# Splitting g tiles one and two points ahead of their products, and deferring parts of w_in's sums, in a fused attention, MoE and gated-layer kernel

## The chip, the cores and the metric

The kernel runs on one core of one Trainium2 chip. The metric is device time in microseconds (us) for one launch; lower is better.

## The reference, cut to what matters

```
kv  = einsum('bhsd,bhse->bhde', k, v);  o = einsum('bhsd,bhde->bhse', q, kv)   # B=8 H=8 S=576 D=64
x   = o / rms(o) * g_norm               # laid out as 4608 rows of 512
e   = argmax(x @ w_gate)                # one of 8 experts for each row
x   = gate_w * (relu(x[e] @ w1[e]) @ w2[e])          # 512 -> 1024 -> 512
h   = x @ w_in                          # 512 -> 2048
g   = h * cos(h)
out = g @ w_out                         # 2048 -> 512, float32
```

## The kernel before, in words

**Precision.** A float32 operand is split in two fp32r tiles, a high part (a ScalarE copy, which rounds) and a low part (the value minus the high part). A product is three passes: high by high, high by low, low by high, as the constant `PASS` says.

**Stages.** The attention part and the routing fill the first 138 us of the trace. The experts r = 0 to 7 follow, in order of size (`emit_f1`, `emit_f2`; L289 and L302 are their matmuls, L291 and L292 the two evictions of the first). From about 677 us on comes the last layer, here called the second half.

**Conversions under the experts.** `w_in` and `w_out` come as 64-bit words. `prep_unit` turns one 128x512 piece into its high and low parts in three steps: VectorE takes exponent and mantissa apart, ScalarE scales (L861, L863), GpSimd multiplies (L864, L865). The generator `prep_units` is advanced one step by each `prep()`, and `prep()` stands between the experts' tiles. The layer with `w_in` uses seven products for a 2x2 block product (sums and differences of blocks take the place of an eighth), so `w_in` also needs four sums per pair of pieces: GpSimd makes them (L886 to L889), ScalarE copies their high parts (L894), VectorE subtracts for the low parts (L895), and GpSimd's queue stores them to `win` in DRAM (L896). This happens eight times, for c = 0 to 7.

**The second half.** A step (p, q) works on a pair p of 512-row groups ("quads") and a block of 2x128 hidden columns. Pair 0 has four steps on one quad, with matmuls of 256 columns; pairs 1 to 4 have eight steps each on two quads: 36 steps in all. In a step TensorE runs the seven products `emit_prod(p, q, 0..6)` (L1174, six 512-column matmuls each from pair 1 on), into the three banks of `ph` and the one of `pt`. VectorE adds them up to four h tiles, C22, C11, C21 and C12 (L1271 to L1310; ScalarE copies product 0 at L1260 and product 4 at L1294, GpSimd adds the latter at L1295). `emit_cos` reduces the argument on VectorE (L1185, L1186, L1188) and takes the cosine on ScalarE (L1190, L1191); `emit_g` multiplies (L1194).

A finished g tile is kept in one of 19 `gslots` until its turn in the list `gq`. From pair 1 on, `gq` takes C11 and C21 of all eight q, for the first quad of the pair, and then C22 and C12, for the second. There are four points in each step, behind products 1, 3, 5 and 6. At each, `emit_split()` takes the next tile of `gq`, if its g is there: ScalarE writes the high part to `gg` (L1207), VectorE the low part (L1208). `second()` right behind it emits the tile's twelve matmuls with `w_out` (L1222). `gg_ring` has three entries. When a quad has all its terms, `emit_rows` copies its four 128-row results out of PSUM (L1233, L1235) and scatters them to `out` (L1236).

All engines run in the order in which the program is written (`manual_schedule`). GpSimd's queue carries the loads of `wi` (L990, five ring entries) and `wo` (L999, four) besides its arithmetic; a load stands behind the product that frees its entry. In the last step of a pair `y_split` makes the operands of the next pair, two ScalarE copies (L971) and two GpSimd subtractions (L972) for each product.

Of the kernel before, what the change touches and what calls it, by code (L numbers as in the profile page):

```python
# [8 lines left out]
F32 = mybir.dt.float32  # L9
# [4 lines left out]
AF = mybir.ActivationFunctionType  # L14
ALU = mybir.AluOpType
# [17 lines left out]
def fused_kernel(  # L33
# [13 lines left out]
    nc = tc.nc  # L47
    P = 128
    B, H, S, D = q.shape
    NT, DM = out.shape  # L50
# [28 lines left out]
    win = dram.tile([C2 // 2, P, 7, 2, 2, P], F32, name="win")  # L79
# [42 lines left out]
    def load_q(b):  # L122
# [24 lines left out]
        out=tri8, in0=iota_e[:, :, None].to_broadcast([P, E, E]),  # L147
        in1=iota_e[:, None, :].to_broadcast([P, E, E]), op=ALU.is_gt)
# [69 lines left out]
    def split_plain(t, d, engine=nc.vector):  # L218
        nc.scalar.activation(d[:, 0], t, AF.Copy)
        engine.tensor_tensor(out=d[:, 1], in0=t, in1=d[:, 0], op=ALU.subtract)  # L220
# [604 lines left out]
    def next_cd():  # L825
        n_cd[0] += 1
        return cds[(n_cd[0] - 1) % len(cds)]

    def prep_unit(i):
        load_raw()  # L830
        t = raws[i]
        d = next_cd()
        if not wide:
            split_plain(t, d)
            yield
            yield
            yield
            return d
        w = t.bitcast(I32).rearrange("p (n two) -> p n two", two=2)
        lo, hi = w[:, :, 0], w[:, :, 1]  # L840
        ex = cpool.tile([P, 512], I32, tag="c0", name="c0")
        nc.vector.tensor_scalar(out=ex, in0=hi, scalar1=0x7FF00000, scalar2=None,
                                op0=ALU.bitwise_and)
        sc = cpool.tile([P, 512], I32, tag="c1", name="c1")
        nc.vector.tensor_scalar(out=sc, in0=hi, scalar1=3, scalar2=0x3F800000,
                                op0=ALU.logical_shift_left, op1=ALU.bitwise_and)
        yield
        nc.vector.scalar_tensor_tensor(out=sc, in0=hi, scalar=-0x40000000, in1=sc,
                                       op0=ALU.bitwise_and, op1=ALU.bitwise_or)
        ef = cpool.tile([P, 512], F32, tag="c2", name="c2")  # L850
        nc.vector.scalar_tensor_tensor(out=ef, in0=ex, scalar=float(0x38100000),
                                       in1=sc.bitcast(F32), op0=ALU.is_ge, op1=ALU.mult)
        nc.vector.tensor_scalar(out=ex, in0=hi, scalar1=9, scalar2=0x7FF,
                                op0=ALU.logical_shift_right, op1=ALU.bitwise_and)
        yield
        nc.vector.tensor_scalar(out=sc, in0=hi, scalar1=0x1FF, scalar2=15,
                                op0=ALU.bitwise_and, op1=ALU.logical_shift_left)
        nc.vector.scalar_tensor_tensor(out=sc, in0=lo, scalar=17, in1=sc,
                                       op0=ALU.logical_shift_right, op1=ALU.bitwise_or)
        mf = cpool.tile([P, 512], F32, tag="c3", name="c3")  # L860
        nc.scalar.activation(mf, ex, AF.Copy, scale=2.0 ** -11, bias=1.0)  # L861
        ml = cpool.tile([P, 512], F32, tag="c4", name="c4")
        nc.scalar.activation(ml, sc, AF.Copy, scale=2.0 ** -35)  # L863
        nc.gpsimd.tensor_tensor(out=d[:, 0], in0=mf, in1=ef, op=ALU.mult)  # L864
        nc.gpsimd.tensor_tensor(out=d[:, 1], in0=ml, in1=ef, op=ALU.mult)  # L865
        yield
        return d


    def prep_units():  # L870
        G = nc.gpsimd
        for c in range(C2 // 2):
            da = yield from prep_unit(2 * c)
            db = yield from prep_unit(2 * c + 1)
            wa = cpool.tile([P, 2, 256], F32, tag="c3", name="wa")
            wb = cpool.tile([P, 2, 256], F32, tag="c4", name="wb")
            for d, w in ((da, wa), (db, wb)):
                G.tensor_tensor(out=w.rearrange("p a n -> p (a n)"), in0=d[:, 0].bitcast(F32),
                                in1=d[:, 1].bitcast(F32), op=ALU.add)
            for d, slots in ((da, (0, 4)), (db, (None, 5))):  # L880
                for h, o in enumerate(slots):
                    if o is not None:
                        G.dma_start(win[c][:, o].rearrange("p t k f -> p t (k f)"),
                                    d.bitcast(F32)[:, :, 256 * h:256 * h + 256])
            yield
            G.tensor_tensor(out=wb[:, 1], in0=wb[:, 0], in1=wb[:, 1], op=ALU.add)  # L886
            G.tensor_tensor(out=wb[:, 0], in0=wa[:, 0], in1=wb[:, 0], op=ALU.subtract)
            G.tensor_tensor(out=wa[:, 0], in0=wb[:, 1], in1=wa[:, 0], op=ALU.subtract)
            G.tensor_tensor(out=wa[:, 1], in0=wa[:, 1], in1=wa[:, 0], op=ALU.subtract)  # L889
            yield  # L890
            for i, w in enumerate((wa, wb)):
                sd = next_cd().rearrange("p t n -> p (t n)").rearrange(
                    "p (a t n) -> p a t n", a=2, t=2)
                nc.scalar.activation(sd[:, :, 0], w, AF.Copy)  # L894
                nc.vector.tensor_tensor(out=sd[:, :, 1], in0=w, in1=sd[:, :, 0], op=ALU.subtract)  # L895
                G.dma_start(  # L896
                    (win[c][:, 2:4] if i else win[c][:, 1:7:5]).rearrange("p a t k f -> p a (t k f)"),
                    sd.bitcast(F32).rearrange("p a t n -> p a (t n)"))
            yield
        for i in range(C2):  # L900
            d = yield from prep_unit(C2 + i)
            G.dma_start(wout[i], d.bitcast(F32))
# [99 lines left out]
    gq, wo_seq = [], []  # L1002
    for q in range(NQ // 2):
        for names, fs in ((("C22", "C21"), (2 * q + NQ, 2 * q + 1 + NQ)),
                          (("C11", "C12"), (2 * q, 2 * q + 1))):
            n = len(wo_seq)
# [138 lines left out]
    reg2_s.close()  # L1145
    reg4 = ctx.enter_context(tc.tile_pool(name="reg4", bufs=1, reuse_waits="tile"))
    wk2 = ctx.enter_context(tc.tile_pool(name="wk2", bufs=2, reuse_waits="tile"))
    gslots = [reg4.tile([P, 512], F32, name=f"g{i}") for i in range(19)]
    stage2 = [reg4.tile([P, 512], F32, name=f"y{i}") for i in range(4)]
    wo = [reg4.tile([P, 2, 512], F32R, name=f"wo{i}") for i in range(WO)]  # L1150
    gg_ring = [reg4.tile([P, 2, 512], F32R, name=f"gg{i}") for i in range(3)]
# [43 lines left out]
        ready.add(key)  # L1195

    n_split = [0]
    waiting = []

    def emit_split():  # L1200
        u = gq[n_split[0]] if n_split[0] < len(gq) else None
        if u is None or u["key"] not in ready:
            return
        gg = gg_ring[n_split[0] % len(gg_ring)]
        n_split[0] += 1
        t = gs.pop(u["key"])
        nc.scalar.activation(gg[:, 0], t, AF.Copy)  # L1207
        nc.vector.tensor_tensor(out=gg[:, 1], in0=t, in1=gg[:, 0], op=ALU.subtract)  # L1208
        gslots.append(t)
        waiting.append((u, gg))  # L1210

    def emit_g2(u, gg, ts=range(4)):
        g = u["g"]
        if g not in acc:
            acc[g] = [ps_a("acc") for _ in range(4)]
        for col, t, item in u["cols"]:
            if t not in ts:
                continue
            wv = wo[item % WO]
            for a, b in PASS:  # L1220
                n = hits[g, t] = hits.get((g, t), 0) + 1
                nc.tensor.matmul(acc[g][t], lhsT=gg[:, a, col * P:(col + 1) * P],  # L1222
                                 rhs=wv[:, b, :], start=(n == 1), stop=(n == 3 * C2))
            if hits[g, t] == 3 * C2:
                emit_rows(g, t)
        if 3 in ts:
            for _ in range(u["n_wo"]):
                load_wo()

    def emit_rows(g, t):  # L1230
        o = wk2.tile([P, DM], F32, tag="yo", name="oo", bufs=4)
        if t % 2:
            nc.scalar.activation(o, acc[g][t], AF.Copy)  # L1233
        else:
            nc.vector.tensor_copy(o, acc[g][t])  # L1235
        sc = nc.gpsimd.indirect_dma_start(  # L1236
            out=out, out_offset=bass.IndirectOffsetOnAxis(
                ap=ctok[:, 4 * g + t:4 * g + t + 1], axis=0),
            in_=o, in_offset=None)
        tc.declare_no_dep(sc.ins, group="rows",  # L1240
                          reason="the rows are a permutation: no two scatters share one")
        tc.add_to_no_dep_group("rows", sc.ins)
        nc.gpsimd.memset(spare, 0.0)

    def second():
        if waiting:
            emit_g2(*waiting.pop(0))

    prev = None
# [79 lines left out]
    second()  # L1329
    emit_g(prev + ("C12",))  # L1330
    while n_split[0] < len(gq):
        emit_split()
        if n_split[0] < len(gq) and len(waiting) > 1:
            second()
    while len(waiting) > 2:
        second()
    for i, ts in ((0, (0, 1)), (1, (0, 1)), (0, (2,)), (1, (2,)), (0, (3,)), (1, (3,))):
        emit_g2(*waiting[i], ts)

# [28 lines left out]
```

## Time and profile before

| | |
|---|---|
| median of three runs | 1836.54 us (1829.53 to 1836.8) |
| the profiled execution | 1835.83 us, its span 1834.0 us |
| busy | PE 1479.6, DVE 1108.8, ACT 662.3, POOL 743.5 us |
| granted TensorE clock, mean | 0.911 |

PE is TensorE (matmul), DVE is VectorE, ACT is ScalarE, POOL is GpSimd. A row of the line table or of the timeline gives line, engine, operation, `output<-inputs`, shape and count; `[2.87 <-ACT gg L1207]` says that the engine sat idle for 2.87 us before it and that this instruction ended the wait. Matmuls overlap, so the ends shown for them are modelled; their starts are read.

### The profile page before, as it was taken

The numbers are of one execution on the slowest core, as the hardware profiler recorded it, in microseconds if no ns is written. First come the engines' busy times: TensorE is split into PE (matmuls) and PEld (weight loads), VectorE is DVE, ScalarE is ACT, GpSimd is POOL, SyncE is SP. The second block draws the span as 40 slices with busy tenths as digits, with TensorE's granted clock in tenths as the row PEclk, the third lists the DMA queues.
The fourth block names the chain that finished last, engine by engine and source line by source line (L and its number), as shares of the span: only waits on it lengthen the run. The fifth ranks groups of instructions, "written<-read, shape, count | busy, mean of one in ns | idle before, by whom it ended". The sixth has DMA issues, their size and how long they took to land.

```text
span 1834.0 us, 22411 instructions
## 1 busy us (share of the span) xinstructions
PE 1479.6 (81%) x7959; PEld 1238.1 (68%) x7959; DVE 1108.8 (60%) x1848; ACT 662.3 (36%) x1308; POOL 743.5 (41%) x869
## 2 busy tenths in 40 slices
PE   7977989989899986677766588886887876888888
PEld 6867879879898985565555466664655655566666
DVE  3987656656788815556666556555555654655651
ACT  5863334434444432323323323233322323323331
POOL 1445456766765652642133412325313334122122
PEclk9989989999999997889887799887989888998999
DMA  9954446656666667465443444544545443445435
GB/s 326 346 178 142 125 155 203 188 161 203 192 217 209 197 182 218 140 200 160 127 120 105 137 141 140 155 129 129 157 132 152 134 120 110 146 132 151 137 96 168
DMA packets 186055, 300.76 MB, mean 164 GB/s; under 512 B 18772, under 2 KB 125316, under 8 KB 184912
## 3 DMA queue, kind: packets, MB, share of 16 engines
q0 software_dynamic: 59392, 191.64, 35.3%
q1 hardware_dynamic: 116624, 97.58, 17.2%
q10 hardware_dynamic: 9920, 10.03, 1.6%
q8 instruction: 65, 1.06, 0.3%
q14 instruction: 54, 0.44, 0.1%
HBM read 247.22 MB, written 51.98 MB: 163 GB/s over the span
## 4 chain that ended last, share of the span: by engine, by line
PE 25%; DVE 19%; ACT 10%; issue 4%; POOL 3%; DMA 1%; POOLq 0%; another core or an unknown queue 0%; DVEq 0%; ACTq 0%
PE acc L1222 17%; PE pr L1174 8%; DVE g L1188 4%; DVE g L1186 4%; DVE gg L1208 3%; ACT g L1190 3%; ACT g L1191 3%; ACT gg L1207 3%; DVE ni L1185 2%; DVE g L1194 2%; POOL xreg L972 1%; DVE ha L1299 1%; DVE hb L1283 1%; ACT p L1294 1%; ACT hb L1260 1%
## 5 line engine op out<-in xcount | busy, mean ns | idle before, releaser
L1222 PE MATMUL acc<-wo,gg 128*128 128x512 f32 x1728 | 532.0, 460 | 239.2 <-ACT gg L1207 198.6
L1222 PEld LDWEIGHTS acc<-wo,gg 128*128 128x128 f32 x1728 | 366.3, 221 | 392.7 <-ACT gg L1207 239.6
L1208 DVE TENSOR_TENSOR gg<-g,gg 128x512 fp32r<-128x512 f32 x144 | 143.6, 998 | 311.2 <-ACT gg L1207 311.2
L999 POOL DMA_DIRECT2D wo<-wout x144 | 79.7, 554 | 529.1 <-PE acc L1222 516.6
L1190 ACT ACTIVATE g<-g 128x512 f32<-128x512 f32 x144 | 90.6, 629 | 499.6 <-DVE g L1188 499.6
L289 PE MATMUL hp<-xreg,wA 128*128 128x352 f32 (+7 forms) x1536 | 232.5, 311 | 34.0 <-DVE wB L292 32.4
L289 PEld LDWEIGHTS hp<-xreg,wA 128*128 128x128 f32 x1536 | 222.9, 194 | 41.0 <-DVE wB L292 39.2
L302 PE MATMUL yp<-wB,wA 128*128 128x352 f32 (+7 forms) x1536 | 232.4, 311 | 13.6 <-ACT yo L309 12.0
L302 PEld LDWEIGHTS yp<-wB,wA 128*128 128x128 f32 x1536 | 222.8, 194 | 15.2 <-ACT yo L309 13.3
L1174 PE MATMUL pr<-wA,wi 128*128 128x512 f32 (+1 forms) x912 | 194.4, 364 | 13.7 <-DMA wi<-win 9.6
L1174 PE MATMUL pr<-xreg,wi 128*128 128x512 f32 x768 | 197.6, 404 | 7.2 <-ACT p L1294 7.2
L1174 PEld LDWEIGHTS pr<-wA,wi 128*128 128x128 f32 x912 | 157.4, 199 | 42.8 <-issue 9.8
L1174 PEld LDWEIGHTS pr<-xreg,wi 128*128 128x128 f32 x768 | 149.7, 195 | 44.4 <-ACT p L1294 7.6
L990 POOL DMA_DIRECT2D wi<-win x128 | 69.1, 540 | 164.6 <-PE pr L1174 164.1
L1188 DVE SCALAR_TENSOR_TENSOR g<-ni,g 128x512 f32<-128x512 int32 x144 | 111.7, 776 | 4.9
L1191 ACT ACTIVATE g<-g,half_pi 128x512 f32<-128x512 f32 x144 | 104.1, 723 | 4.7
L208 POOL TENSOR_TENSOR wA<-w1s,wA 128x512 fp32r<-128x512 f32 x64 | 84.4, 1324 | 46.7 <-ACT wA L207 46.0
L292 DVE SCALAR_TENSOR_TENSOR wB<-hp,wB 128x352 fp32r<-128x352 f32 (+7 forms) x128 | 57.3, 470 | 66.2 <-ACT wB L291 66.0
L1207 ACT ACTIVATE gg<-g 128x512 fp32r<-128x512 f32 x144 | 85.7, 617 | 26.9 <-PE acc L1222 26.6
L1279 DVE TENSOR_TENSOR ha<-ha,pr 128x512 f32<-128x512 f32 x36 | 24.7, 686 | 106.8 <-PE pr L1174 106.8
L291 ACT ACTIVATE wB<-hp 128x352 fp32r<-128x352 f32 (+7 forms) x128 | 51.4, 420 | 74.8 <-PE hp L289 68.8
L1260 ACT ACTIVATE hb<-pr 128x512 f32<-128x512 f32 x36 | 21.3, 592 | 156.6 <-PE pr L1174 156.6
(213 smaller groups left out, 2022.9 us busy)
## 6 DMA issues: line engine op xcount, KB each, us to landing
wo<-wout POOLq DMA_DIRECT2D x144, 512.0 KB
wi<-win POOLq DMA_DIRECT2D x124, 512.0 KB
w1s<-in_moe_w_dram SPq DMA_DIRECT2D x64, 256.0 KB
w2s<-in_moe_w_dram SPq DMA_DIRECT2D x64, 256.0 KB
xs<-xo SPq DMA_DIRECT2D x16, 512.0 KB
raww<-in_moe_w_in_dram SPq DMA_DIRECT2D x16, 512.0 KB
win<-xreg POOLq DMA_DIRECT2D x16, 512.0 KB
raww<-in_moe_w_out_dram SPq DMA_DIRECT2D x16, 512.0 KB
```

The costliest lines, as they stand in the source:

```text
L208: nc.gpsimd.tensor_tensor(out=d[:, 1], in0=t, in1=d[:, 0], op=ALU.subtract)
L289: nc.tensor.matmul(ps, lhsT=wv[:, a, kk, :], rhs=xT[:, b, kk, sl], start=(i == 0 and kk == 0), stop=(i == 2 and kk == KD - 1))
L302: nc.tensor.matmul(ps, lhsT=wv[:, a, kk % 4, :], rhs=hT[:, kk, b, sl], start=(n == 0), stop=(n == 3 * C1 - 1))
L999: nc.gpsimd.dma_start(wo[n % WO], wout[wo_seq[n]])
L1174: nc.tensor.matmul(ps, lhsT=w[:, a, kk, :], rhs=y[:, b, kk, :], start=(n == 0), stop=(n == 5))
L1186: nc.vector.scalar_tensor_tensor(out=r, in0=ni, scalar=-PI2_HI, in1=h, op0=ALU.mult, op1=ALU.add)
L1188: nc.vector.scalar_tensor_tensor(out=r, in0=ni, scalar=-PI2_LO, in1=r, op0=ALU.mult, op1=ALU.add)
L1190: nc.scalar.activation(r, r, AF.Abs)
L1191: nc.scalar.activation(r, r, AF.Sin, scale=-1.0, bias=half_pi)
L1207: nc.scalar.activation(gg[:, 0], t, AF.Copy)
L1208: nc.vector.tensor_tensor(out=gg[:, 1], in0=t, in1=gg[:, 0], op=ALU.subtract)
L1222: nc.tensor.matmul(acc[g][t], lhsT=gg[:, a, col * P:(col + 1) * P], rhs=wv[:, b, :], start=(n == 1), stop=(n == 3 * C2))
```

## The change

In the second half `emit_split` now writes the high part of the next tile and the low part of the tile before it; `second()` emits the products of the tile before that, once more than two tiles are on their way. So a tile's high part is taken two points ahead of its products, and its low part one point ahead. There are 20 `gslots` instead of 19, and three buffers for the result rows `oo` instead of four. The end of the program is written to suit.

In the conversions, the two high and low parts of w_in's sums of one c (ScalarE, VectorE) are put on a list, and the third step of the next unit emits them; their stores to `win` come behind that unit's GpSimd multiplications. The step of the generator that they had to themselves is gone, so the conversions take 8 steps fewer in all.

```diff
+    pend, stores = [], []
+    def flush(l):
+        while l:
+            l.pop(0)()
     def prep_unit(i):
...
         nc.vector.scalar_tensor_tensor(out=sc, in0=lo, scalar=17, in1=sc, ...
+        flush(pend)
+        d = next_cd()
         mf = cpool.tile([P, 512], F32, tag="c3", name="c3")
...
         nc.gpsimd.tensor_tensor(out=d[:, 1], in0=ml, in1=ef, op=ALU.mult)
+        flush(stores)
         yield
         return d
+    def sum_parts(c, i, w):
+        sd = next_cd().rearrange(...)
+        nc.scalar.activation(sd[:, :, 0], w, AF.Copy)
+        nc.vector.tensor_tensor(out=sd[:, :, 1], in0=w, in1=sd[:, :, 0], op=ALU.subtract)
+        stores.append(lambda: nc.gpsimd.dma_start(...))
...
             for i, w in enumerate((wa, wb)):
-                sd = next_cd()...
-                nc.scalar.activation(sd[:, :, 0], w, AF.Copy)
-                nc.vector.tensor_tensor(out=sd[:, :, 1], in0=w, in1=sd[:, :, 0], op=ALU.subtract)
-                G.dma_start(...)
-            yield
+                pend.append(lambda c=c, i=i, w=w: sum_parts(c, i, w))
...
-    gslots = [reg4.tile([P, 512], F32, name=f"g{i}") for i in range(19)]
+    gslots = [reg4.tile([P, 512], F32, name=f"g{i}") for i in range(20)]
...
+    lows = []
-    def emit_split():
+    def emit_hi():
...
         nc.scalar.activation(gg[:, 0], t, AF.Copy)
+        lows.append((u, gg, t))
+    def emit_low():
+        u, gg, t = lows.pop(0)
         nc.vector.tensor_tensor(out=gg[:, 1], in0=t, in1=gg[:, 0], op=ALU.subtract)
         gslots.append(t)
         waiting.append((u, gg))
+    def emit_split():
+        emit_hi()
+        if len(lows) > 1:
+            emit_low()
...
-        o = wk2.tile([P, DM], F32, tag="yo", name="oo", bufs=4)
+        o = wk2.tile([P, DM], F32, tag="yo", name="oo", bufs=3)
...
     def second():
-        if waiting:
+        if len(waiting) + len(lows) > 2:
             emit_g2(*waiting.pop(0))
...
     while n_split[0] < len(gq):
+        second()
         emit_split()
-        if n_split[0] < len(gq) and len(waiting) > 1:
-            second()
-    while len(waiting) > 2:
-        second()
+    emit_g2(*waiting.pop(0))
+    emit_low()
```

## Rows read from the trace of the kernel before

**Rows 1.** The page: busy time by engine, and the chain that ended last.
```profile
PE 1479.6 (81%) x7959; PEld 1238.1 (68%) x7959; DVE 1108.8 (60%) x1848; ACT 662.3 (36%) x1308; POOL 743.5 (41%) x869
...
PE 25%; DVE 19%; ACT 10%; issue 4%; POOL 3%; DMA 1%; POOLq 0%; another core or an unknown queue 0%; DVEq 0%; ACTq 0%
```

**Rows 2.** Waits by pair, 712 us to the end: total, times, longest.
```profile
DVE gg L1208 <- ACT gg L1207: 309.9, 109, 9.3
...
PE acc L1222 <- ACT gg L1207: 192.6, 73, 11.0
...
PE acc L1222 <- DVE gg L1208: 38.9, 39, 3.3
...
ACT gg L1207 <- PE acc L1222: 26.6, 13, 2.8
```

**Rows 3.** Timeline, PE alone, from 1118 us: one step of pair 2.
```profile
1118.06 1.56 PE L1174 MATMUL pr<-wA,wi 128*128 128x512 f32 x6
...
1122.10 3.33 PE L1222 MATMUL acc<-wo,gg 128*128 128x512 f32 x12 [1.08 <-ACT gg L1207]
1125.27 2.97 PE L1174 MATMUL pr<-xreg,wi 128*128 128x512 f32 x12
1128.08 2.88 PE L1222 MATMUL acc<-wo,gg 128*128 128x512 f32 x12
1130.80 1.56 PE L1174 MATMUL pr<-xreg,wi 128*128 128x512 f32 x6
...
1142.06 3.30 PE L1222 MATMUL acc<-wo,gg 128*128 128x512 f32 x12 [2.87 <-ACT gg L1207]
```

**Rows 4.** Windows: that step, and a stretch of the end.
```profile
1118.10:1145.20 27.10, 22.43 (x92) 16.41 (x90) 15.37 (x25) 8.46 (x14) 5.64 (x9) 1.00 0.51 146
1790.00:1826.00 36.00, 35.65 (x156) 29.21 (x156) 9.01 (x13) 7.28 (x13) 7.49 (x15) 1.00 0.59 173
```

**Rows 5.** Windows of the second half: PE, PEld, DVE, ACT, POOL busy; clock; DMA; GB/s.
```profile
676.60:700.30 23.70, 14.09 (x85) 13.91 (x86) 6.71 (x9) 2.43 (x4) 7.67 (x11) 0.72 1.03 292
700.30:808.80 108.50, 75.03 (x386) 62.32 (x386) 69.40 (x90) 35.14 (x59) 53.00 (x57) 0.83 0.60 176
808.80:864.10 55.30, 45.14 (x170) 33.41 (x169) 32.47 (x52) 17.60 (x29) 15.84 (x25) 0.93 0.52 152
864.10:983.30 119.20, 87.06 (x331) 67.91 (x330) 74.45 (x111) 34.40 (x56) 29.90 (x41) 0.86 0.43 120
983.30:1061.10 77.80, 48.29 (x157) 34.83 (x156) 47.93 (x63) 27.39 (x46) 36.23 (x40) 0.76 0.43 130
1061.10:1235.60 174.50, 145.40 (x542) 106.91 (x540) 102.57 (x160) 53.03 (x88) 46.70 (x68) 0.92 0.50 142
1235.60:1283.40 47.80, 31.27 (x92) 22.20 (x91) 24.13 (x26) 15.00 (x26) 25.54 (x25) 0.79 0.43 126
1283.40:1491.50 208.10, 172.11 (x631) 126.80 (x630) 119.73 (x186) 62.65 (x104) 57.34 (x85) 0.91 0.50 143
...
1539.30:1742.60 203.30, 168.39 (x631) 123.90 (x630) 117.09 (x185) 61.63 (x102) 48.82 (x78) 0.93 0.49 144
1742.60:1834.00 91.40, 75.07 (x307) 58.68 (x306) 33.22 (x51) 23.02 (x38) 20.33 (x36) 0.94 0.44 132
```

**Rows 6.** Timeline, DVE and POOL in the last step of pair 2.
```profile
1250.00 4.00 DVE L1208 TENSOR_TENSOR gg<-g,gg 128x512 fp32r<-128x512 f32 x1 [6.58 <-ACT gg L1207]
...
1250.95 2.49 POOL L972 TENSOR_TENSOR xreg<-y,xreg 128x512 fp32r<-128x512 f32 x2
...
1287.73 0.69 DVE L1208 TENSOR_TENSOR gg<-g,gg 128x512 fp32r<-128x512 f32 x1 [4.49 <-ACT gg L1207]
```

**Rows 7.** Waits by pair under the experts, 150 to 712 us.
```profile
ACT xreg L894 <- POOL wa L889: 57.0, 8, 8.8
...
DVE xreg L895 <- ACT xreg L894: 49.6, 8, 8.4
...
PE hp L289 <- DVE wB L292: 32.4, 21, 6.7
```

More of the change, by code (lines that the diff above doesn't have):

```diff
@@ L831, in prep_unit @@
         t = raws[i]
-        d = next_cd()
         if not wide:
+            flush(pend)
+            d = next_cd()
             split_plain(t, d)
+            flush(stores)
             yield
@@ L859, in prep_unit @@
                                        op0=ALU.logical_shift_right, op1=ALU.bitwise_or)
+        flush(pend)
+        d = next_cd()
         mf = cpool.tile([P, 512], F32, tag="c3", name="c3")
@@ L865, in prep_unit @@
         nc.gpsimd.tensor_tensor(out=d[:, 1], in0=ml, in1=ef, op=ALU.mult)
+        flush(stores)
         yield
         return d
+    def sum_parts(c, i, w):
+        sd = next_cd().rearrange("p t n -> p (t n)").rearrange("p (a t n) -> p a t n", a=2, t=2)
+        nc.scalar.activation(sd[:, :, 0], w, AF.Copy)
+        nc.vector.tensor_tensor(out=sd[:, :, 1], in0=w, in1=sd[:, :, 0], op=ALU.subtract)
+        stores.append(lambda: nc.gpsimd.dma_start(
+            (win[c][:, 2:4] if i else win[c][:, 1:7:5]).rearrange("p a t k f -> p a (t k f)"),
+            sd.bitcast(F32).rearrange("p a t n -> p a (t n)")))
     def prep_units():
@@ L891, in prep_units @@
             for i, w in enumerate((wa, wb)):
-                sd = next_cd().rearrange("p t n -> p (t n)").rearrange(
-                    "p (a t n) -> p a t n", a=2, t=2)
-                nc.scalar.activation(sd[:, :, 0], w, AF.Copy)
-                nc.vector.tensor_tensor(out=sd[:, :, 1], in0=w, in1=sd[:, :, 0], op=ALU.subtract)
-                G.dma_start(
-                    (win[c][:, 2:4] if i else win[c][:, 1:7:5]).rearrange("p a t k f -> p a (t k f)"),
-                    sd.bitcast(F32).rearrange("p a t n -> p a (t n)"))
-            yield
+                pend.append(lambda c=c, i=i, w=w: sum_parts(c, i, w))
         for i in range(C2):
```

## The prediction

> **What bounds the kernel now.** I read the page first. PE is busy for 81% of the span, but the chain that ended last runs over PE for only 25% and over DVE and ACT for 29% [rows 1]: the other engines' latency stands in TensorE's way, not a lack of TensorE work elsewhere. The view of the waits says where. In the second half PE sits idle for 192.6 us until ACT has written a tile's high part and for 38.9 us until DVE has written its low part, 231.5 us in all. DVE itself waits 309.9 us for that same high part, and everything behind that subtraction on DVE waits with it [rows 2].
>
> The timeline of one step shows the pattern. TensorE does its products, comes to the twelve `w_out` matmuls of a point, and stops for 1.08 or 2.87 us because ACT, which is in order, has only just passed the cosines ahead of that copy [rows 3]. The tile's g is old by then: in pairs 2 to 4 a tile waits in its slot for steps. So what is late is the split, not its input. The same rows give TensorE's pace where nothing is missing: twelve product matmuls from 1125.27 to 1128.08, so 1.40 us for a product of six, and twelve `w_out` matmuls from 1128.08 to 1130.80, 2.72 us. A step has seven products and four tiles: 7 x 1.40 + 4 x 2.72 = 20.7 us. This one took 27.1 us at a granted clock of 1.00, with DVE busy for 15.4 us and ACT for 8.5 [rows 4]. Nobody is full.
>
> The windows add the rest: six such steps take 174.5 us (29.1 each), seven take 208.1 and seven 203.3 (29.7 and 29.0), at clocks of 0.91 to 0.93 [rows 5]. The clock is below its upper level, 2.4 GHz, where PE has stood still; in the end of the program 156 matmuls follow one another for 36 us at 1.00, 0.229 us each [rows 4]. So a step loses some 6 us to waits and 2 to matmuls at the lower level, 1.2 GHz, behind them.
>
> **The change, part by part: the second half.** No instruction is added or dropped; the order changes. I laid the new order out by hand from the start of product 0, with TensorE never waiting: the tiles' matmuls (a, b, c, d for the four points) begin at 2.8, 8.3, 13.9 and 18.0 us, products 2, 5 and 6 end at 6.9, 13.9 and 18.0. DVE works without a break from product 5 to the second low part of the next step (add, cosine of C21, g, cosine of C11, low, add, g, cosine of C12, g, low, add, low: 18 instructions at 0.61 us, which is 15.37 over 25 [rows 4], 11.6 us with the seams, to 4.7 us in the next step), waits 2.2 us for product 2, works 5.2 us on the other eight, and waits 1.7 us for product 5. The low parts are there at 3.4, 4.7, 12.2 and 19.5 us; their products are the tiles at b, c, d and the next a, so each is 4 to 9 us early. The high parts come at 3.9, 6.1, 13.6 and 20.9 us, 8 us or more ahead of their products. The wait that is added is the ring's: a high part at a point goes into the entry whose matmuls were emitted one point before. At b it holds ACT from about 3.9 to 5.5 us, 1.6 us; at a, c and d those matmuls are over when ACT comes. Behind it on ACT is the cosine of C22, whose input is there only at 11.4 us, so nobody waits for that. PSUM banks come free 5 us or more ahead.
>
> So a regular step becomes bound by TensorE's own 20.7 us. I add 0.9 us for quad ends, for the third `oo` buffer (the fourth row's copy waits for the first row's scatter; ACT has that time in 21 us with 8.5 busy) and for GpSimd's sums of the next pair: **21.6**. Bounds: 20.7, and 27.1 for the best step now.
>
> By stretches of [rows 5], in their order:
> - Steps 1 to 3 of pair 0: 108.5 us with PE busy for 75.0, so 33.5 idle. Here tiles are ready late and GpSimd is busy for 53. I take back 70% of the idle time: **23** (0 to 46, the latter with the clock's loss).
> - First two steps of pair 1: 55.3 us; their 168 matmuls need 39. I take 42: **13**.
> - Next five steps: 119.2 us. Only two tiles a step become ready, so TensorE needs 15.3 us a step; DVE needs about 14.5 with its waits in line. I take 18.2, since GpSimd's sums fall here: **28** (5 to 42).
> - The step with the seven `y_split` of pair 1 and the one behind it: 77.8 us, need 36. GpSimd has 36 us of work here. I take 52: **26** (0 to 38).
> - Six, seven and seven regular steps at 21.6: 174.5 to 130, 208.1 to 151, 203.3 to 151: 44 + 57 + 52 = **153** (44 to 172).
> - The last steps of pairs 2 and 3, 47.8 us each (one row stands for both): GpSimd is busy for 25.5 of them, and it is in order with `y_split`. I take 31: 17 each, **34** (0 to 45).
> - The end: 91.4 us, 306 matmuls of 70 us and 8 us behind the last. I take 81: **10**.
>
> Sum: 23 + 13 + 28 + 26 + 153 + 34 + 10 = 287 us.
>
> At the `y_split` steps a rule has to be weighed. The same subtraction took 0.69 us alone, and 4.00 us where two GpSimd subtractions, ending at 1253.44, ran under it; it ended 0.56 us behind them [rows 6]. The Trainium skill, page "SBUF — State Buffer", section "Who interferes with whom", says that a VectorE instruction with two SBUF inputs and a GpSimd instruction that reads SBUF exclude one another for the whole of the first to start. The trace agrees. By that rule GpSimd's and DVE's work add up there rather than overlap, and the 31 us would be a floor; without it about 27.
>
> **The conversions.** ACT waits for GpSimd's sums eight times, 57.0 us, DVE behind it 49.6, and behind DVE stand the experts' evictions, for which PE waits 32.4 us, at most 6.7 at a time [rows 7]. Two steps later the sums should be done or nearly: GpSimd is now up to 8.8 us behind [rows 7], and two steps, about two tiles of an expert, are of that size. The same two copies and two subtractions remain, and the next unit's scaling must now wait for the subtractions to read their tiles, about 1.4 us of ACT; the stores move behind two multiplications on GpSimd's queue, and `win` is first read by the second half. The eight steps saved only end the conversions sooner. Not all of the 32.4 us is these eight stalls, but clock comes back with them: **24** (0 to 50).
>
> **Sum.** 287 + 24 = 311. Against the profiled execution's own time, 1835.8 us, that is 1525 us; the median is 0.7 us above it, which changes nothing.
>
> **Rivals.**
> - DVE becomes the bound: its 15.4 us plus two waits in line, stretched where GpSimd's arithmetic overlaps, make a step of 24.6 and not 21.6. For it: little slack between the waits (2.2 and 1.7 us). Against it: TensorE tolerates 4 us of lateness. 20 x 3, with 10 in the other stretches: 1595. Chance 0.19.
> - GpSimd's chain holds: pair 0 and the `y_split` steps keep their time, the five steps of pair 1 half of their gain: 23 + 26 + 34 + 14 = 97 less: 1622. For it: GpSimd's 53, 36 and 25 us of work there. Against it: PE's waits in these rows end with `gg` too. Chance 0.11.
> - The loads come late: a step brings 3.9 MB, 182 GB/s at 21.6 us against 142 now. For it: one queue carries them. Against it: 292 GB/s at 677 us, 173 at the end without a wait that matters. At 160 GB/s a step takes 24.5: 1583. Chance 0.04.
> - Slower: the ring of three closes a loop. If ACT comes to a high part over two points (10 us) late, TensorE waits for it and ACT for TensorE at every point, and a step takes 32 us: 20 x 2.5 more, about 1885. Against it: ACT has 12 us free in a step, and that wait is 26.6 us in all now [rows 2]. Chance 0.02.
> - The change does not do what it says: tiles become ready only at their point, so that nothing is ahead, and the conversions' waits only move: 1836. The five steps of pair 1 are bound by readiness; the twenty regular ones are not. Chance 0.02.
>
> **How the numbers follow.** The forecast has 0.62: 1525. All lower bounds together would give about 1415; I do not expect TensorE's floor in every stretch, so the range begins at 1455, some two thirds of the way. It ends at 1620, which takes in the first and third rival and half of the second. Left out are the other half, the last two and the tails: under 0.2. A measurement of this kernel tells 0.5% (9 us) from no change. Faster 0.96, same 0.02, slower 0.02.
>
> **What would show it.** Right: PE's wait for `gg` falls from 231 to under 50 us, the regular steps stand at 21 to 22 us at a clock near 1.00, DVE's wait for the high part is nearly gone and its idle time ends with PE; ACT's wait at L894 falls from 57 to under 15. Wrong: regular steps above 24 us with DVE or `wi`/`wo` loads ending PE's waits, or `y_split` steps still near 48.

## The result, and the profile after

The changed kernel takes 1504.8 us (median of four runs, 1500.76 to 1508.87) against 1833.05 of the kernel before beside it: a ratio of 0.821 [0.818, 0.824], some 328 us less where 311 were forecast. The profiled execution took 1508.87 us, with a span of 1506.5.

The page first, its busy times and the chain that ended last, to be held against [rows 1]:

```profile
PE 1356.9 (90%) x7959; PEld 1188.3 (79%) x7959; DVE 1145.8 (76%) x1848; ACT 664.9 (44%) x1308; POOL 755.5 (50%) x869
...
PE 34%; DVE 12%; POOL 3%; issue 3%; ACT 2%; DMA 1%; POOLq 0%; another core or an unknown queue 0%; DVEq 0%; ACTq 0%
```

The counts are the same; TensorE is busy for 123 us less, for the greater part because the same matmuls ran more often at the upper clock (worked out below). The chain has moved from VectorE and ScalarE (29% to 14%) to TensorE. DVE and POOL rose by 37 and 12 us without one instruction more: they now get in each other's way more often, which the experiments come to.

The view of the waits, 652 us to the end, beside [rows 2] (total, times, longest):

```profile
ACT gg L1221 <- PE acc L1245: 44.4, 26, 2.1
DVE gg L1226 <- ACT gg L1221: 38.8, 44, 2.9
...
PE acc L1245 <- DVE gg L1226: 29.2, 8, 5.7
...
PE pr L1186 <- ACT p L1317: 15.6, 3, 7.2
```

TensorE's wait for the high part (192.6 us) is gone from the list and its wait for the low part fell to eight stalls. VectorE's wait for the high part went from 309.9 to 38.8. The wait that the change adds is the first row: ScalarE waits for the ring entry, at most 2.1 us at a time. At the end of the program VectorE waits behind it, 2.0 us at each tile, and these stalls are the larger part of its 38.8; TensorE has no wait in this view that ends with that copy. The last row has grown: three stalls of product 1 for the eviction of product 4, where there was one of 7.2 us before.

TensorE's timeline over one step of pair 2 has no idle time in it, where [rows 3] had two stalls:

```profile
976.20 1.56 PE L1186 MATMUL pr<-wA,wi 128*128 128x512 f32 x6
...
979.00 2.89 PE L1245 MATMUL acc<-wo,gg 128*128 128x512 f32 x12
981.74 2.97 PE L1186 MATMUL pr<-xreg,wi 128*128 128x512 f32 x12
984.54 2.89 PE L1245 MATMUL acc<-wo,gg 128*128 128x512 f32 x12
...
990.08 2.89 PE L1245 MATMUL acc<-wo,gg 128*128 128x512 f32 x12
992.82 1.56 PE L1186 MATMUL pr<-wA,wi 128*128 128x512 f32 x6
994.22 2.89 PE L1245 MATMUL acc<-wo,gg 128*128 128x512 f32 x12
996.94 1.57 PE L1186 MATMUL pr<-wA,wi 128*128 128x512 f32 x6
```

From the step's start the four tiles begin at 2.80, 8.34, 13.88 and 18.02 us, which is the layout made by hand (2.8, 8.3, 13.9, 18.0). The step takes 20.74 us. VectorE sits idle only twice in it (the other seams are under 0.3 us):

```profile
983.34 0.69 DVE L1302 TENSOR_TENSOR ha<-ha,pr 128x512 f32<-128x512 f32 x1 [2.42 <-PE pr L1186]
...
990.28 0.69 DVE L1322 TENSOR_TENSOR ha<-ha,pr 128x512 f32<-128x512 f32 x1 [1.86 <-PE pr L1186]
```

The windows of the second half, stretch by stretch as in [rows 5] (columns as there); the stretch of 208.1 us is cut in two here, its first step by itself:

```profile
652.40:673.80 21.40, 14.02 (x84) 13.84 (x85) 6.57 (x9) 2.43 (x4) 7.61 (x11) 0.68 1.10 321
673.80:746.30 72.50, 59.32 (x362) 52.33 (x361) 70.10 (x76) 30.73 (x52) 49.41 (x50) 0.93 0.70 213
746.30:791.80 45.50, 41.67 (x170) 33.40 (x169) 37.54 (x58) 19.39 (x32) 18.53 (x27) 0.92 0.69 210
791.80:878.60 86.80, 80.41 (x331) 63.69 (x330) 80.33 (x118) 35.88 (x59) 32.30 (x45) 0.96 0.61 183
878.60:934.40 55.80, 41.58 (x157) 31.75 (x156) 47.04 (x57) 25.17 (x43) 32.86 (x33) 0.88 0.53 152
934.40:1060.80 126.40, 125.07 (x542) 101.30 (x541) 106.38 (x163) 53.90 (x89) 51.47 (x76) 1.00 0.69 205
1060.80:1081.60 20.80, 20.80 (x91) 16.79 (x90) 20.56 (x21) 10.81 (x19) 14.33 (x14) 1.00 0.61 173
1081.60:1115.90 34.30, 24.89 (x92) 19.19 (x91) 25.30 (x34) 14.64 (x25) 17.84 (x21) 0.80 0.56 169
1115.90:1242.70 126.80, 125.09 (x542) 101.33 (x541) 105.09 (x160) 52.32 (x88) 51.10 (x76) 1.00 0.71 208
1242.70:1263.40 20.70, 20.70 (x91) 16.79 (x90) 20.46 (x22) 10.77 (x19) 16.01 (x15) 1.00 0.50 148
1263.40:1421.40 158.00, 149.76 (x632) 120.67 (x631) 122.86 (x193) 68.04 (x113) 60.02 (x89) 0.96 0.66 193
1421.40:1506.50 85.10, 75.75 (x331) 61.60 (x329) 34.46 (x55) 23.65 (x39) 21.65 (x38) 0.98 0.52 155
sum 854.10, PE 779.07 PEld 632.68 DVE 676.69 ACT 347.72 POOL 373.13; mean PE 64.92 PEld 52.72 DVE 56.39 ACT 28.98 POOL 31.09
```

The same sum for the kernel before, from 676.6 us on:

```profile
sum 1157.40, PE 893.10 PEld 673.09 DVE 651.89 ACT 347.27 POOL 366.94; mean PE 893.10 PEld 673.09 DVE 651.89 ACT 347.27 POOL 366.94
```

So the second half is 303 us shorter. TensorE's idle time went from 264 to 75 us (1157.4 - 893.1 and 854.1 - 779.1), 189 us; the other 114 us are the same matmuls in less busy time. Most of that is the granted clock, 0.88 on average before and 0.95 after. By the trace's clock records TensorE was busy at the lower level, 1.2 GHz in place of 2.4, for 210 us before and for 52 after; half of the difference, 79 us, is an estimate of what the clock gave back. The other 35 us are not due to the clock. The step of [rows 4] stood at 1.00 throughout, and TensorE was busy in it for 22.43 us, against 20.74 in the step above: twelve `w_out` matmuls that start behind a wait take 3.33 or 3.30 us there, and 2.88 without one [rows 3]. So a wait costs more than the idle time that the view shows. And the second half starts 24.2 us earlier (652.4 against 676.6). Two things stand out: the six and six regular steps at a clock of 1.00, and the first step of pair 3, 34.3 us at 0.80; those of pairs 2 and 4 take 32.4 and 33.2 us. One row has to be read with care: in steps 1 to 3 of pair 0 there are 362 matmuls against 386, and in the end 331 against 307. With two points of lead the `w_out` matmuls of two tiles, 24 in all, have moved out of pair 0 and come out at the end.

### The profile page after: what moved, and what is told of

Read it like the earlier page. It is cut to its first block, busy times and chain, and to the rows that moved or that the text cites. A ratio compares the mean times of both kernels' runs of the same rounds, so it can differ in the third digit from the quotient of the medians.

```text
span 1506.5 us, 22532 instructions
## 1 busy us (share of the span) xinstructions
PE 1356.9 (90%) x7959; PEld 1188.3 (79%) x7959; DVE 1145.8 (76%) x1848; ACT 664.9 (44%) x1308; POOL 755.5 (50%) x869
## 4 chain that ended last, share of the span: by engine, by line
PE 34%; DVE 12%; POOL 3%; issue 3%; ACT 2%; DMA 1%; POOLq 0%; another core or an unknown queue 0%; DVEq 0%; ACTq 0%
PE acc L1245 19%; PE pr L1186 15%; DVE ni L1197 3%; DVE g L1200 3%; DVE g L1198 2%; POOL xreg L984 2%; DVE g L1206 1%; DMA wi<-win 1%; DVE ha L1322 1%; DVE gg L1226 1%; POOL y L979 0%; ACT wA L983 0%; ACT g L1203 0%; ACT g L1202 0%; POOL wo L1011 0%
## 5 line engine op out<-in xcount | busy, mean ns | idle before, releaser
L1245 PE MATMUL acc<-wo,gg 128*128 128x512 f32 x1728 | 431.2, 400 | 30.8 <-DVE gg L1226 29.2
L1245 PEld LDWEIGHTS acc<-wo,gg 128*128 128x128 f32 x1728 | 331.8, 193 | 110.4 <-DVE gg L1226 35.6
L289 PE MATMUL hp<-xreg,wA 128*128 128x352 f32 (+7 forms) x1536 | 228.1, 308 | 26.5 <-DVE wB L292 25.0
L289 PEld LDWEIGHTS hp<-xreg,wA 128*128 128x128 f32 x1536 | 219.7, 192 | 32.5 <-DVE wB L292 30.7
L302 PE MATMUL yp<-wB,wA 128*128 128x352 f32 (+7 forms) x1536 | 227.5, 306 | 1.8 <-DVE xreg L273 1.5
L302 PEld LDWEIGHTS yp<-wB,wA 128*128 128x128 f32 x1536 | 217.1, 189 | 3.3 <-DVE xreg L273 2.5
L1226 DVE TENSOR_TENSOR gg<-g,gg 128x512 fp32r<-128x512 f32 x144 | 126.1, 876 | 39.1 <-ACT gg L1221 38.8
L1200 DVE SCALAR_TENSOR_TENSOR g<-ni,g 128x512 f32<-128x512 int32 x144 | 120.0, 833 | 4.9
L1197 DVE TENSOR_SCALAR ni<-hb 128x512 int32<-128x512 f32 x72 | 53.7, 745 | 20.2 <-POOL hb L1318 20.2
L1318 POOL TENSOR_TENSOR hb<-hb,p 128x512 f32<-128x512 f32 x36 | 49.0, 1361 | 32.0 <-ACT p L1317 30.0
```

The lines of the kernel that those rows point to most:

```text
L289: nc.tensor.matmul(ps, lhsT=wv[:, a, kk, :], rhs=xT[:, b, kk, sl], start=(i == 0 and kk == 0), stop=(i == 2 and kk == KD - 1))
L302: nc.tensor.matmul(ps, lhsT=wv[:, a, kk % 4, :], rhs=hT[:, kk, b, sl], start=(n == 0), stop=(n == 3 * C1 - 1))
L1197: nc.vector.tensor_scalar(out=ni, in0=h, scalar1=INV_2PI, scalar2=None, op0=ALU.mult)
L1200: nc.vector.scalar_tensor_tensor(out=r, in0=ni, scalar=-PI2_LO, in1=r, op0=ALU.mult, op1=ALU.add)
```

## The experiments

Each edit is made to the changed kernel; each ratio is against the kernel before, timed on the same chip.

**The two parts apart.** The first kernel keeps the splitting of the second half and takes the deferral back; the second keeps the deferral and takes the splitting back.

```diff
 # first: prep_unit and prep_units as before
-                pend.append(lambda c=c, i=i, w=w: sum_parts(c, i, w))
+                sd = next_cd()...; nc.scalar.activation(...); nc.vector.tensor_tensor(...); G.dma_start(...)
+            yield
 # second: 19 gslots, 4 oo buffers, emit_split, second and the end as before
-        if len(waiting) + len(lows) > 2:
+        if waiting:
```

> Only the second half's change; the conversions are those of before. Theory (the two parts add up; the windows of the changed kernel give the second half 303 us of the gain and the stages ahead of it 24): 1530 us, the second half 854 us long as in the changed kernel. Rival (the parts depend on each other, for example because a later start of the conversions' end moves loads): under 1520 or over 1545.

> Only the deferred sums; the second half is that of before. Theory: 1809 us, 24 less than before, ScalarE's wait for GpSimd's sums (57.0 us before) under 15, the second half unchanged at 1157 us. Rival (the stalls under the experts only move): 1825 or more.

Measured: 1534.05 us (0.835 [0.832, 0.838]) and 1809.24 us (0.984 [0.981, 0.988]) against 1836.13. The gains, 302 and 27, add up to the 328 of both. In the first kernel ScalarE's wait for the sums stands as before (56.9 us, eight times); in the second it is 2.0 us, in two stalls.

**Is one point of lead enough?** In the first kernel high and low part of a tile are both emitted one point ahead of its products; in the second the high part one point ahead and the low part at the point of the products. The end of the program is written to suit in both.

```diff
 # both one ahead
-        if len(lows) > 1:
+        if lows:
             emit_low()
-        if len(waiting) + len(lows) > 2:
+        if len(waiting) > 1:
 # high one ahead, low at its own point
-        if len(waiting) + len(lows) > 2:
+        if waiting:
```

> The changed kernel with both parts of a tile taken at the same point, one point ahead of its products. Theory (what counts is that no engine that is in order waits for another inside a point; here VectorE still waits at each point for the high part that ScalarE takes behind its cosines): a regular step is set by VectorE's chain, worked out by hand as 22.8 to 23.5 us instead of 20.75, so 1545 to 1560 us. Rival (any lead of the split over the products is enough): 1505 us, steps at 20.75.

> The changed kernel with the high part one point ahead of the products and the low part at the point of the products. Theory: VectorE no longer waits for ScalarE, but TensorE's third matmul of a tile waits for the low part at points a and d (by the hand schedule the low part is there 0.7 and 1.5 us late), so regular steps of 22 to 24 us, 1530 to 1570 us, with TensorE's waits ended by the low part. Rival (only the high part's lead counts): 1505 us.

Measured: 1589.76 us (0.866 [0.863, 0.868]) and 1625.68 us (0.886 [0.883, 0.888]), 85 and 121 us more than the change. Both directions were as the theory had them; the sizes were too small. The waits of the first, 650 us to the end, show which engine comes late:

```profile
DVE gg L1226 <- ACT gg L1221: 218.2, 107, 9.2
...
PE acc L1245 <- ACT gg L1221: 65.4, 32, 7.5
```

VectorE still stands behind ScalarE's copy (218.2 us, against 38.8 after the change), since it comes to the low part at the same point as ScalarE to the high one. In the second it is the low part (first row, from the waits), and a regular step shows it at its last point:

```profile
PE acc L1245 <- DVE gg L1226: 131.8, 40, 9.8
...
1015.55 0.69 DVE L1226 TENSOR_TENSOR gg<-g,gg 128x512 fp32r<-128x512 f32 x1
...
1016.29 2.57 PE L1245 MATMUL acc<-wo,gg 128*128 128x512 f32 x10 [1.10 <-DVE gg L1226]
```

Two of the twelve matmuls, those of the first result that need only the high part of g, had started; the ten others waited for VectorE, which had an add, two cosine reductions and a g before the subtraction. Plain steps took 21.5 to 22.5 us in the first, under the 22.8 to 23.5 expected, and 22.1 in the second; the larger part of the loss lies in pair 1, at quad ends and at ends of pairs, where the expectations had left the steps as they were. Each of the two points is therefore needed: one so that ScalarE is ahead of VectorE, one so that VectorE is ahead of TensorE.

**How much slack has VectorE?** The low part is computed two and three times over, the same value each time, so each step carries four and eight more VectorE instructions of 0.61 us.

```diff
     def emit_low():
         u, gg, t = lows.pop(0)
+        nc.vector.tensor_tensor(out=gg[:, 1], in0=t, in1=gg[:, 0], op=ALU.subtract)   # once, or twice
         nc.vector.tensor_tensor(out=gg[:, 1], in0=t, in1=gg[:, 0], op=ALU.subtract)
```

> The changed kernel with every low part computed twice (the same values once more, one VectorE instruction of 0.69 us more at each of the four points). Theory (TensorE is the bound of a regular step, VectorE has about 4 us to spare in 20.75): regular steps stay at 20.75 to 21 us; only where VectorE is close to being the bound already (pair 1, the steps with y_split) time is lost, 15 to 30 us: 1520 to 1535. Rival (VectorE is the bound): 2.76 us in each of 36 steps, 1600.

> The changed kernel with every low part computed three times (two more VectorE instructions at each point, 5.5 us a step). Theory: VectorE now needs 16.8 + 5.5 = 22.3 us of a 20.75 us step and becomes the bound: regular steps of 22.3 to 23.5 us, with TensorE's waits ended by VectorE; 1570 to 1610 us in all. Rival (the slack is larger than the hand schedule has it): regular steps still at 20.75, under 1550.

Measured: 1540.5 us (0.838 [0.836, 0.840]), just above what was expected, and 1598.71 us (0.870 [0.869, 0.872]), within it. A regular step of the first:

```profile
987.00:1007.70 20.70, 20.70 (x92) 16.86 (x91) 18.41 (x30) 8.66 (x15) 5.64 (x10) 1.00 0.70 191
```

VectorE is busy for 18.4 us and the step still takes TensorE's 20.7; the 36 us lost are for the most part in pairs 0 and 1 and in the last two steps of pairs 2 and 3. With three, plain steps take 20.7 to 21.9 us, less than the 22.3 to 23.5 expected, and a single step in pairs 2 and 3 over 30 (31.6 and 30.4). A stretch of 30 us over parts of two steps of pair 2 shows VectorE with hardly a gap:

```profile
1030.00:1060.00 30.00, 25.90 (x110) 20.04 (x109) 29.25 (x47) 12.11 (x21) 8.54 (x14) 1.00 0.57 171
```

So the rival that VectorE is the bound was wrong for the change: four more instructions, 2.4 us, cost a plain step nothing. Eight, 4.9 us, cost it up to 1.2, so the slack is some 3.7 us by estimate, and beyond it the rival is right.

**The stalls at the ends of pairs.** A large part of what is left of the loss is in the first steps of pairs 2, 3 and 4. This is the timeline of the one of pair 3, at 1081.6 us, after the change:

```profile
1084.26 2.49 POOL L979 TENSOR_TENSOR y<-yst,y 128x512 f32<-128x512 f32 x2
...
1085.57 0.63 ACT L983 ACTIVATE xreg<-y 128x512 fp32r<-128x512 f32 x1 [4.56 <-POOL y L979]
...
1087.32 0.58 ACT L1317 ACTIVATE p<-pr 128x512 f32<-128x512 f32 x1
...
1087.95 2.93 PE L1186 MATMUL pr<-wA,wi 128*128 128x512 f32 x6 [4.76 <-ACT p L1317]
...
1090.47 3.79 DVE L1197 TENSOR_SCALAR ni<-hb 128x512 int32<-128x512 f32 x1 [6.17 <-POOL hb L1318]
...
1096.37 4.43 PE L1245 MATMUL acc<-wo,gg 128*128 128x512 f32 x10 [4.64 <-DVE gg L1226]
```

`y_split` number 5 waits on ScalarE for GpSimd's subtraction (4.56 us); behind it stands the eviction of product 4 (L1317), for whose bank product 1 of the next step waits (4.76 us); and the GpSimd addition behind that eviction feeds C11, which VectorE waits for (6.17 us) ahead of the low part that TensorE needs (4.64 us). The theory: `y_split` 4 and 5 stand in front of that eviction, and moving them behind point c takes the stall away. The rival: GpSimd's arithmetic itself is what is late.

```diff
         ps = emit_prod(p, q, 4)
-        if p < NPAIR and last and p > 0:
-            y_split(p + 1, 4)
         p4 = emit_prod(p, q, 5)
-        if p < NPAIR and last:
-            y_split(p + 1, 5)
...
         emit_split()
         second()
+        if p < NPAIR and last:
+            if p > 0:
+                y_split(p + 1, 4)
+            y_split(p + 1, 5)
```

> The changed kernel with y_split of products 4 and 5 of the next pair, in the last step of a pair, emitted behind point c and not around product 5. Theory (what is left over the floor at the ends of pairs is one chain: ScalarE's copy of product 4 stands behind copies of y_split that wait for GpSimd, and with it TensorE's next bank, GpSimd's sum for C11 and VectorE's cosine): the three steps of 32 to 34 us fall to 22 to 27, TensorE's 15.6 us of waits for that copy are gone; 1465 to 1490 us. Rival (GpSimd's sheer work there sets the time): the chain only moves, 1500 to 1510.

Measured: 1502.8 us (0.819 [0.817, 0.820]), no change, and the theory fell. TensorE's wait for L1317 (15.6 us) is indeed gone, but its wait for the low part rose from 29.2 to 41.1. The timeline says why:

```profile
1074.25 8.04 DVE L1206 TENSOR_TENSOR g<-hb,g 128x512 f32<-128x512 f32 x1
1074.28 2.55 POOL L984 TENSOR_TENSOR xreg<-yst,xreg 128x512 fp32r<-128x512 f32 x2
...
1076.78 2.51 POOL L979 TENSOR_TENSOR y<-yst,y 128x512 f32<-128x512 f32 x2
...
1079.25 2.49 POOL L984 TENSOR_TENSOR xreg<-y,xreg 128x512 fp32r<-128x512 f32 x2
...
1087.15 4.46 PE L1245 MATMUL acc<-wo,gg 128*128 128x512 f32 x10 [9.19 <-DVE gg L1226]
```

One multiplication of VectorE, 0.68 us elsewhere, took 8.04 us while GpSimd did six subtractions back to back, from 1074.28 to 1081.74; it ended 0.55 us behind the last of them. VectorE is not waiting for a result there, it is shut out. That is the mechanism of [rows 6], at twice the length.

**Two remedies.** If GpSimd's unbroken arithmetic shuts VectorE out, spreading it should help, and giving it to VectorE should help more. The first kernel puts `y_split` 4 behind point c and leaves 5 and 6 to the points a and b of the next pair's first step, still on GpSimd. The second leaves the order and does the low parts of `y_split` 1 to 6 on VectorE, behind the next point.

```diff
 # spread (pairs 1 to 3)
+        if p > 1 and q == 0:
+            y_split(p, 5)      # point a;  y_split(p, 6) likewise at b
 # low parts on VectorE
-            nc.gpsimd.tensor_tensor(out=o[:, 1], in0=t, in1=o[:, 0], op=ALU.subtract)
+            late.append(lambda o=o, t=t: nc.vector.tensor_tensor(
+                out=o[:, 1], in0=t, in1=o[:, 0], op=ALU.subtract))
...
         emit_split()
+        flush(yl)
```

> y_split of product 4 behind point c of the last step of a pair, and those of products 5 and 6 behind points a and b of the next pair's first step, the subtractions still on GpSimd. Theory (at the ends of pairs VectorE is shut out while GpSimd subtracts back to back; over two steps both together are some 54 us of work in 41.5, and TensorE tolerates 4 us of lateness): 8 us or a little less are lost at each end instead of 13: 1480 to 1495 us. Rival (products 5 and 6 of the new pair then wait for their operands): 1505 or more, with TensorE's waits ended by L984.

> The twelve subtractions of y_split in the last step of a pair done by VectorE, behind the next point, and not by GpSimd. Theory (the time at the ends of pairs is the time that GpSimd's subtractions, 1.25 us each, keep VectorE out; VectorE does the same one in 0.69): VectorE has 8.3 us more to do, ends the step some 4 us late, which TensorE tolerates, and works that off in the next: the steps of 32 to 34 us fall to 21 to 24, 1465 to 1480 us. Rival (VectorE is full there, so that its 8.3 us are paid whole; GpSimd's time was hidden): 1505 to 1530.

Measured: 1491.21 us (0.811 [0.808, 0.815]), as expected, and 1482.43 us (0.806 [0.803, 0.810]), just above it. The windows of the second, the last step of pair 2 and the first of pair 3:

```profile
1048.00:1069.80 21.80, 21.02 (x92) 16.63 (x90) 20.29 (x27) 12.37 (x23) 8.87 (x10) 1.00 0.59 178
1069.80:1095.10 25.30, 22.47 (x91) 17.93 (x92) 23.97 (x39) 11.92 (x21) 8.43 (x12) 0.93 0.69 216
```

47.1 us for the two, against 55.1 after the change, though VectorE got twelve instructions more: it takes 1.28 us for two of these subtractions, GpSimd 2.5, and in these two steps no instruction of VectorE takes more than 3.01 us. The first steps of pairs 2 to 4 take 23.2, 25.3 and 26.8 us, where 21 to 24 was expected.

**All of it together.** The last kernel does every low part of `y_split` for pairs 1 to 4 on VectorE, also those that are taken during pair 0, and puts `y_split` 4 and 5 behind point c.

```diff
+        if p < NPAIR and last:
+            if p > 0:
+                y_split(p + 1, 4, yl)
+            y_split(p + 1, 5, yl)
...
-                y_split(1, 2 * q - 2)
-                y_split(1, 2 * q - 1)
+                y_split(1, 2 * q - 2, yl)
+                y_split(1, 2 * q - 1, yl)
...
-                y_split(p + 1, 0)
+                y_split(p + 1, 0, yl)
```

> The kernel with y_split's low parts on VectorE, with three more edits: y_split of products 4 and 5 behind point c (so that product 4's copy does not stand behind GpSimd's subtraction for product 5), and the low parts of y_split in pair 0 and of product 0 on VectorE too. Theory (what is left at the ends of pairs is ScalarE's copy of product 4 behind that chain, 7.9 us of waits, and in pair 0 VectorE shut out by GpSimd): 1460 to 1475 us, the steps behind the ends at 21 to 23, steps 2 and 3 of pair 0 under 24. Rival (VectorE's own work is the bound there): 1480 to 1490.

Measured: 1470.11 us (1467.49 to 1473.1), 0.802 [0.800, 0.804], the fastest kernel here, and as expected. Steps 2 and 3 of pair 0 take 23.7 and 21.4 us, under 24. The first steps of pairs 3 and 4 take 23.1 and 23.0, but that of pair 2 still 27.3, where 21 to 23 was expected. No run separates what each of the added edits gave. Its page:

```profile
PE 1347.4 (92%) x7959; PEld 1182.9 (81%) x7959; DVE 1138.1 (78%) x1904; ACT 664.7 (45%) x1308; POOL 680.0 (46%) x813
```

VectorE has 56 instructions more than after the change (1904 against 1848) and is busy for 7.7 us less.

**Two side parts of the change.** One kernel gives back the fourth `oo` buffer, with 19 `gslots`. The other puts the empty step of the conversions back, so that only the deferral is left and their number of steps is as before.

```diff
 # first
-    gslots = [... for i in range(20)]
+    gslots = [... for i in range(19)]
-        o = wk2.tile([P, DM], F32, tag="yo", name="oo", bufs=3)
+        o = wk2.tile([P, DM], F32, tag="yo", name="oo", bufs=4)
 # second, behind the loop over (wa, wb)
+            yield
```

> The changed kernel with 19 gslots and four buffers for the result rows, as before (20 and four do not fit in the memory together). Theory (the third buffer's 18.8 us of ScalarE waits lie beside TensorE's work, and the twentieth slot is slack): 1500 to 1510 us, ScalarE's wait for the scatter gone. Rival (ScalarE's wait at quad ends reaches TensorE): 1485 to 1495 us; (the slot was needed): above 1515.

> The changed kernel with the eight steps of the conversions' generator kept (an empty one for each c), the sums' parts still deferred. Theory (the gain under the experts comes from the deferral alone): 1500 to 1510 us, ScalarE's wait for GpSimd's sums as short as in the changed kernel. Rival (a part comes from the conversions being done eight steps sooner): 1515 to 1530.

Measured: 1504.38 us (0.818 [0.815, 0.822]) and 1502.26 us (0.818 [0.816, 0.820]), both no different from the change. Taken together, the third buffer costs nothing and the twentieth slot gives nothing: ScalarE's wait for the scatter, 18.8 us in seven stalls after the change, is gone in the first and the time stays. And the gain of the conversions is the deferral's, not the eight steps'.

## Why the prediction was right

**What bounds it.** Right. The split was late, not its input: with the lead, TensorE's waits for `gg` fell from 231.5 to 29.2 us. In the two experiments with less lead they are 74.3 and 140.4 us (65.4 + 8.9 and 131.8 + 8.6), and the kernel is 85 and 121 us longer than with the change.

**The regular step.** Right in its mechanism, and a little timid. The layout by hand gave VectorE two waits of 2.2 and 1.7 us; the trace has 2.42 and 1.86. The low parts were due at 3.4, 4.7, 12.2 and 19.5 us; VectorE ended them at 3.1, 4.7, 12.2 and 19.7. A plain step takes 20.74 us, the floor, and six steps with a quad's end in them 126.4 us, 21.1 each, where 21.6 was taken.

**The stretches**, gains in us, forecast and measured (differences of [rows 5] and the windows above):

```
                                     forecast   measured
first step of pair 0                     0          2
steps 1 to 3 of pair 0                  23         36
first two of pair 1                     13         10
next five                               28         32
y_split step of pair 1, next one        26         22
six regular steps of pair 2             44         48
last steps of pairs 2 and 3             34         54
seven steps of pair 3, of pair 4        57 + 52    47 + 45
end                                     10          6
second half                            287        303
conversions                             24         24
```

One term was mis-sized by itself: pair 0. There 70% of the 33.5 idle us was taken back, 23 us, and the idle time in fact fell by 20.3, to 13.2. But TensorE's busy time also fell, from 75.0 to 59.3 us, and the value taken had nothing for that. Some 6 us of it only moved: at 0.23 to 0.28 us each, that is what the 24 matmuls cost that now come out at the end, so an even account would have about 30 us in pair 0 and 12 at the end, beside 23 and 10. The other 9 or 10 us go with the clock, 0.93 against 0.83, whose return was named with the upper bound and left out of the value taken. Pair 0's 7 are thus about half of the 16 between 287 and 303. The other terms err by 2 to 4 us both ways, those from the last step of pair 2 on taken together.

The prediction put the loss of the best regular step, 27.1 us against 20.7, at some 6 us of waits. The idle time in it is 4.7 us (27.10 - 22.43); the rest is matmuls that took longer behind a wait, at the upper clock. The sum is not touched by this, since it went from the step's whole time to 21.6.

**The ends of pairs** were right in their sum and wrong in their place. The last steps were to keep 31 us each; they took 20.8 and 20.7, and the `y_split` loss came out in the next step, 34.3 us at 1081.6 where the same step took this before:

```profile
1283.40:1314.60 31.20, 24.39 (x92) 17.94 (x91) 17.20 (x27) 9.65 (x16) 10.59 (x17) 0.93 0.54 161
```

TensorE has no idle time in them (20.80 us busy of 20.80): with two points of lead it works there on tiles split earlier, so a late GpSimd shows a step later. From the last step of pair 2 to the seventh of pair 4 the forecast was 507 - 364 = 143 us of gain; measured, 507 - 361 = 146. The rule weighed there held as to the work, not as a floor of that one step: GpSimd's and VectorE's instructions did exclude one another, and the last step of pair 2 and the step behind it took 55.1 us, beside 31 + 21.6 forecast. Moving the subtractions to VectorE was worth 22 us (1504.8 to 1482.4), and the last kernel 35 (to 1470.1).

**The conversions.** The sum was right, 24 by the trace and 27 by the run with them alone; the way was told too narrowly. ScalarE's wait for the sums fell from 57.0 to 2.5 us, and the new one, scaling behind the subtractions, is there:

```profile
ACT c L871 <- DVE xreg L883: 14.7, 8, 3.2
...
ACT xreg L882 <- POOL wa L908: 2.5, 4, 1.6
...
PE hp L289 <- DVE wB L292: 25.0, 21, 3.5
```

It is 14.7 us in eight stalls where 1.4 each, 11 us, was counted. But the path through VectorE's evictions gave 7.4 us only (PE's wait 32.4 to 25.0). ScalarE's own evictions of the second matmuls, which wait in the same queue, gave as much. Before they cost 12.0 us:

```profile
PE yp L302 <- ACT yo L309: 12.0, 4, 3.4
```

After they cost 3.8, on another line. Between 150 us and the second half's start TensorE's idle time fell from 58.4 to 44.1 us and its busy time by 9.9, at a clock of 0.99 against 0.96: 14.3 + 9.9 = 24.2.

**The rivals.** VectorE as the bound: not so, with the slack measured by the doubled and tripled low part. GpSimd's chain: not as it was priced. Pair 0 and the `y_split` steps, which were to keep their time, gave about 30, 22 and 54 us, and the five steps of pair 1 gave 32, where half of 28 was allowed. What the chain still costs the changed kernel is of the size of the 35 us that the last kernel took off. The loads: 205 and 208 GB/s in the regular steps, more than the 182 of the forecast, and TensorE waited 9.3 us for `wi` in all. The ring's loop: ScalarE waited 2.1 us at the most. All of it moved without an effect: no.

**What stays open.** The change leaves TensorE 75 us of idle time in the second half. The last kernel takes 35 us off the time, idle time and slower matmuls together; for what is left, in pair 0, pair 1, the first step of pair 2 and behind the last matmul, no run was made.

## What to carry to other kernels

Where in-order engines hand a tile on (ScalarE, then VectorE, then TensorE), each handover wants a point of lead of its own: with one point for both, or none for the second, a quarter to over a third of the gain was lost. Lay the regular step out by hand against the engine that should set the pace; the seams of such a layout, here 2.2 and 1.7 us, can be read back from the trace, and say which engine would be next. Price a removed stall with the matmuls behind it: here 114 of 303 us came back as busy time, some 79 of them by the clock. And where a lead moves work across the border of a stretch, count the instructions on both sides before comparing.

## What the hardware showed that was not expected

The shutting out is longer than one pair of instructions. The Trainium skill, page "SBUF — State Buffer", section "Who interferes with whom", says that the first to start keeps the shared port pair for the whole instruction. The trace goes further: where GpSimd had six subtractions without a pause, VectorE's multiplication was held through all six (8.04 us for 0.68), not let in between two of them. The two starts shown lie 0.03 us apart, too close to tell which was first.

An instruction of VectorE with one input in SBUF was held up too. The same `tensor_scalar` that takes 0.42 us in the regular step took 3.79 us above at 1090.47, and 3.01 us in the kernel with the low parts on VectorE:

```profile
1061.27 3.01 DVE L1201 TENSOR_SCALAR ni<-hb 128x512 int32<-128x512 f32 x1
1061.45 2.54 POOL L979 TENSOR_TENSOR y<-yst,y 128x512 f32<-128x512 f32 x2
```

At 1090.47 the GpSimd arithmetic that it ran beside began a microsecond later:

```profile
1091.48 2.49 POOL L984 TENSOR_TENSOR wA<-y,wA 128x512 fp32r<-128x512 f32 x2
```

In that microsecond GpSimd was issuing two loads, so what held the instruction at first is open; it ended 0.29 us behind the two subtractions, as it did behind those in the other kernel.

The same section says that `tensor_scalar` can take both port pairs in its fast modes, and so contend; these rows fit that as far as the subtractions go. No run here tried that operation by itself.

At full use, 542 matmuls of 512 columns with their weight loads ran in 125.1 us at a granted clock of 1.00, 0.231 us each, over six steps with 1.3 us of idle time, beside loads at 205 GB/s. The clock did not fall in these six steps.
